# A written order of work up to head 16, weights decoded by half chunks, their remainders subtracted on GpSimd

## The chip, the cores and the metric

The kernel runs on one core of a Trainium2 chip. The metric is device time in microseconds (us). TensorE (PE) multiplies, VectorE (DVE), ScalarE (ACT) and GpSimd (POOL) do elementwise work, and the queue of SyncE (SP) issues most transfers. Each engine takes its instructions in the order in which they stand in its own queue; semaphores hold an instruction until what it needs is there.

## What is computed

A local window attention, followed by a feed-forward network over its output. There are 8 batches of 8 heads; the 512 queries of a head see 32 global keys and the keys at most 32 positions away, and the 32 global queries see all keys.

```python
s_l = np.concatenate([s_lg, np.where(mask, s_ll, -1e9)], axis=-1)
out_l = np.matmul(sm(s_l), np.concatenate([v_g, v_l], axis=2))
out_g = np.matmul(sm(s_g), v_all)
...
h = x @ w_in                      # x: 4608 x 512, w_in: 512 x 2048
r = np.maximum(h, 0.0)
g = s * (r * r) + b
return g @ w_out                  # w_out: 2048 x 512
```

The data are float32. The weights arrive as 64-bit floats; attention data as 32-bit ones.

## The kernel before

Most matmuls run on pairs: a float32 number is written as a rounded high part (`fp32r`) and the remainder, a low part, and three products are summed. So almost every operand is copied rounded on ACT and then subtracted from the original on DVE or POOL.

**Weights.** `w_in` and `w_out` come in 16 chunks each. A chunk k (`weight_load`) is two transfers of 512 KB into one staging tile `wst`: 1024 words of `w_in`, 1024 of `w_out`. `weight_words` turns half a chunk (128x512 numbers) from 64-bit words into pairs in five instructions: ACT rescales the high words (L157), DVE shifts them (L160) and joins the low words' bits to them (L161), ACT rounds the high part into `w_all` (L166), DVE subtracts it from the joined number (L167). These names below are *exponents*, *shift*, *join*, *round* and *subtract*. There are 32 halves.

**Steps.** The loop over j takes one half (256 queries) of one head at a time; "head j" is meant so. The first sixteen (NF = 16) use plain float32 matmuls on PE, the later ones use pairs. For a head: scores on PE into the one PSUM tile `ps_s`; mask and smallest value on DVE (L223, two instructions); exponentials on ACT (L229); a small addition and a reciprocal on DVE (L232, L233); division by the sum (L237 on ACT for one block and L239 on DVE for the other, as `NORM_ACT` says); four transpositions on PE into the one PSUM tile `turned` (L309, L311), a copy back on ACT (L326), and for each second head the product with the values (L339) and its copy to `x` (L347 on DVE, from head 8 on L345 on ACT). After eight heads `x_split` makes a pair of `x` and the feed-forward products can begin: in step j = m + 10 (LAG = 10) `ffn_in(m)` issues 24 matmuls (L515), relu on ACT, square on DVE (L522), a rounded copy on ACT (L529) and the remainder on DVE (L530), and `ffn_out` follows a step later with 12 matmuls (L547). There are 136 m.

**Who sets the order.** The loop is written in order of j, but a scheduler puts the instructions into the queues by its own estimates of time, with priorities: the float32 heads run under a priority 50 places ahead (`AHEAD`). One chunk is decoded at each j from 0 to 15 (`DECODED_AT`). In step j < 10 four matmuls on constants (`keep_busy`, L105) go ahead of the scores; 14 of them stand at the very start. The softmax tile `sm` has two buffers, staging tiles lie in the places of tiles that are used later (`SPOTS`: xs0, xs1 and two places of kq).

Of the kernel before, what the change touches and what calls it, by code (L numbers as in the profile page):

```python
# [48 lines left out]
WARM_UNTIL = 10  # L49
# [3 lines left out]
SPOTS = ["xs0", "xs1", "kq", "kq"] * 2 + ["xs1", "kq", "kq"] * 2 + ["xs1", "kq"]  # L53
DECODED_AT = list(range(16))
BY_HALVES = 16
NORM_ACT = lambda j, blk: j < NF and blk == 0
X_ACT = lambda j: j >= 8
# [4 lines left out]
GL_POOL = lambda m: False  # L62
# [8 lines left out]
def window_attention_then_ffn(ctx: ExitStack, tc: tile.TileContext, qd, qg, kw, vw, vg, qz, qgz, vz, w_in, w_out, sv, bv, out):  # L71
# [75 lines left out]
    def weight_chunk(k):  # L147
        st = staged.pop(k)
        n = 2 if k < BY_HALVES else 1
        for i in range(n):  # L150
            c = 1024 // n
            weight_words(k, st[:, 2 * c * i:2 * c * (i + 1)], slice(c * i, c * (i + 1)))

    def weight_words(k, st, at):
        words = st.rearrange("p (n w) -> p n w", w=2)
        low, high = words[:, :, 0], words[:, :, 1]
        nc.scalar.activation(  # L157
            out=high.bitcast(F32), in_=high.bitcast(F32), func=AF.Prelu, scale=2.0**-112, alpha=2.0**32,
        )
        nc.vector.tensor_scalar(out=high, in0=high, scalar1=3, scalar2=None, op0=ALU.logical_shift_left)  # L160
        nc.vector.scalar_tensor_tensor(  # L161
            out=low, in0=low, scalar=29, in1=high, op0=ALU.logical_shift_right, op1=ALU.bitwise_or,
        )
        m = low.bitcast(F32)
        hi, lo = (w_all[:, i, k].rearrange("p w c -> p (w c)")[:, at] for i in range(2))
# [25 lines left out]

    def split(j):
# [14 lines left out]
    def v_split(j):  # L207
# [3 lines left out]
        nc.scalar.copy(out=vs[:, :, 0, :], in_=rv4)  # L211
# [394 lines left out]
    for j in range(NM + LAG + 2):  # L606
# [12 lines left out]
        if j < NS:  # L619
# [106 lines left out]
```

## Time and profile before

| | |
|---|---|
| time, median of 3 runs | 1012.91 us (1012.5 to 1012.93) |
| the profiled execution: its time, its span | 1012.75 us, 1010.9 us |
| busy in the span: PE, weight loads of PE | 994.8 us (98%), 906.0 us |
| DVE, ACT, POOL | 804.0 us, 695.4 us, 288.5 us |
| granted clock of PE, mean | 0.998 of 2.4 GHz |
| transfers | 82.05 MB; 332, 342 and 278 GB/s in the first three of 40 equal slices, 36 to 106 in most later ones |

The span runs from the first to the last instruction; the time holds 1.85 us more. Engines overlap, so busy times are not to be added. An instruction's record lasts until its result is written; the next of its engine starts a little earlier.

### The profile page before, as it was taken

What the parts mean: (1) busy time and instruction counts of PE and PEld (TensorE: products, weight loads), DVE (VectorE), ACT (ScalarE), POOL (GpSimd) and SP (SyncE); (2) the same over time, 40 slices, a digit from 0 to 9 for tenths busy, and PEclk for the clock granted to TensorE, in tenths of its full rate; (3) what the DMA queues carried; (4) which work ended last, traced back from release to release, by engine and by line L of the source; (5) the groups of instructions that cost most, each with busy time, mean ns of one, the idle gap of its engine ahead of it and who ended that gap; (6) DMA issues with size and microseconds to landing.
All of it is one profiled execution on the core that took longest, in us unless ns stands there. A gap on an engine that the chain in (4) does not pass through costs nothing.

```text
span 1010.9 us, 20088 instructions
## 1 busy us (share of the span) xinstructions
PE 994.8 (98%) x6940; PEld 906.0 (90%) x6942; DVE 804.0 (80%) x2097; ACT 695.4 (69%) x1801; POOL 288.5 (29%) x366
## 2 busy tenths in 40 slices
PE   8699999999999999999999999999999999999998
PEld 5589999999999999999999999999999999999887
DVE  7998678888789778988789789988789788964322
ACT  7997667768677667868677667867678667743222
POOL 1002224424243224424244224424234223401000
PEclk9999999999999999999999999999999999999999
DMA  9982212313132212313132112312132112101000
GB/s 332 342 278 77 73 48 66 93 45 99 45 91 66 65 48 62 106 34 93 49 94 69 58 55 62 98 41 87 44 104 69 55 55 65 62 1 49 23 22 21
DMA packets 63845, 82.05 MB, mean 81 GB/s; under 512 B 7680, under 2 KB 51200, under 8 KB 63744
## 3 DMA queue, kind: packets, MB, share of 16 engines
q1 hardware_dynamic: 63168, 79.46, 25.8%
q8 instruction: 55, 0.90, 0.4%
q10 hardware_dynamic: 576, 1.31, 0.4%
q14 instruction: 46, 0.38, 0.1%
HBM read 71.30 MB, written 9.44 MB: 80 GB/s over the span
## 4 chain that ended last, share of the span: by engine, by line
PE 91%; DVE 4%; ACT 3%; issue 1%; DMA 1%; DVEq 0%; ACTq 0%
PE ps_h L515 36%; PE acc L547 35%; PE ps_s L373 5%; PE ps_o L401 4%; PE turned L311 3%; PE turned L309 3%; PE ps_og L467 2%; PE ps_g L380 1%; PE turned L445 1%; PE ps_s L284 1%; DVE wst L161 1%; PE ps_o L339 1%; DVE sm L223 1%; ACT sm L229 0%; DVE wst L160 0%
## 5 line engine op out<-in xcount | busy, mean ns | idle before, releaser
L515 PE MATMUL ps_h<-xst,w_all 128*128 128x256 f32 x3264 | 437.6, 281 | 1.0 <-ACT xst L500 0.7
L547 PE MATMUL acc<-w_all,g 128*128 128x512 f32 x1632 | 422.3, 396 | 0.0
L515 PEld LDWEIGHTS ps_h<-xst,w_all 128*128 128x128 f32 x3264 | 408.0, 189 | 8.9 <-ACT xst L500 0.9
L547 PEld LDWEIGHTS acc<-w_all,g 128*128 128x128 f32 x1632 | 289.9, 188 | 49.6
L212 POOL TENSOR_TENSOR vs<-rv,vs 128x192 fp32r<-128x192 f32 x112 | 70.8, 632 | 301.2 <-ACT vs L211 288.6
L229 ACT ACTIVATE sm<-sm,nm 128x224 f32<-128x224 f32 x256 | 121.5, 477 | 34.3 <-DVE nm L223 33.0
L522 DVE SCALAR_TENSOR_TENSOR r<-ps_h,s_t,r 128x512 f32<-128x512 f32 x136 | 101.5, 746 | 52.7 <-ACT r L521 50.9
L530 DVE SCALAR_TENSOR_TENSOR g<-r,b_t,g 128x512 fp32r<-128x512 f32 x136 | 111.1, 817 | 38.7 <-ACT g L529 34.6
L204 POOL TENSOR_TENSOR kq<-rq,kq 128x256 fp32r<-128x256 f32 x112 | 91.8, 820 | 161.4 <-ACT kq L203 151.3
L529 ACT ACTIVATE g<-r,b_t 128x512 fp32r<-128x512 f32 x136 | 98.5, 724 | 55.1 <-DVE r L522 54.9
L521 ACT ACTIVATE r<-ps_h 128x512 f32<-128x512 f32 x136 | 81.2, 597 | 67.6 <-PE ps_h L515 57.5
L459 POOL TENSOR_TENSOR vsg<-rvg,vsg 128x320 fp32r<-128x320 f32 x64 | 56.8, 908 | 125.5 <-ACT vsg L458 124.1
L239 DVE TENSOR_SCALAR sm<-sm,nm 128x224 f32<-128x224 f32 x240 | 87.8, 405 | 4.0
L373 PE MATMUL ps_s<-kq 128*128 128x224 f32 x448 | 73.7, 275 | 0.0
L373 PEld LDWEIGHTS ps_s<-kq 128*128 128x128 f32 x448 | 67.1, 190 | 6.1
L390 ACT CAST pt<-turned 128x416 fp32r<-128x416 f32 x112 | 57.4, 513 | 21.6 <-PE turned L311 21.0
L391 DVE TENSOR_TENSOR pt<-turned,pt 128x416 fp32r<-128x416 f32 x112 | 65.5, 585 | 7.0 <-ACT pt L390 6.3
L385 DVE TENSOR_TENSOR sg<-ps_g,tg 32x256 f32<-32x256 f32 (+1 forms) x112 | 48.2, 430 | 22.4 <-ACT tg L384 17.0
L309 PE MATMUL turned<-ident,sm 128*96 128x128 f32 (+1 forms) x256 | 63.7, 274 | 1.8 <-DVE sm L239 1.2
L384 ACT COPY tg<-ps_g 32x256 f32<-32x256 f32 (+1 forms) x112 | 42.1, 376 | 32.3 <-PE ps_g L380 29.6
L311 PE MATMUL turned<-ident,sm 128*128 128x128 f32 x256 | 63.1, 273 | 0.0
L401 PE MATMUL ps_o<-pt,vs 128*128 128x256 f32 x336 | 62.9, 295 | 0.0
(81 smaller groups left out, 1273.6 us busy)
## 6 DMA issues: line engine op xcount, KB each, us to landing
rq<-in_qd SPq DMA_DIRECT2D x112, 128.0 KB, 2.2
rk<-in_kw SPq DMA_DIRECT2D x64, 176.0 KB, 2.3
rv<-in_vw SPq DMA_DIRECT2D x112, 96.0 KB, 1.9
rvg<-in_vg SPq DMA_DIRECT2D x32, 320.0 KB, 3.0
out<-o SPq DMA_DIRECT2D x32, 256.0 KB, 2.2
wst<-in_w_in SPq DMA_DIRECT2D x15, 512.0 KB, 5.2
wst<-in_w_out SPq DMA_DIRECT2D x15, 512.0 KB, 6.0
rv<-in_vz SPq DMA_DIRECT2D x16, 192.0 KB, 4.5
```

Source lines behind the costliest of these rows:

```text
L204: nc.gpsimd.tensor_sub(out=qs[:, 1, :], in0=rq, in1=f32(qs[:, 0, :]))
L229: nc.scalar.activation(out=p, in_=p, func=AF.Exp, bias=nm[:, blk:blk + 1], scale=-1.0, accum_out=ss[:, blk:blk + 1],)
L239: nc.vector.tensor_scalar(out=p, in0=p, scalar1=ss[:, blk:blk + 1], scalar2=1.0, op0=ALU.mult, op1=ALU.mult,)
L309: nc.tensor.transpose(out=p_t[0:n, s0:s0 + P], in_=sm[:, c0:c0 + n], identity=ident)
L311: nc.tensor.transpose(out=p_t[:, o0:o0 + P], in_=sm[:, c0:c0 + P], identity=ident)
L373: nc.tensor.matmul(p_s[:, W * blk:W * blk + W], lhsT=qs[:, a, blk * P:(blk + 1) * P], rhs=ks[:, KEYS[blk]], start=(a == 0), stop=(a == 1),)
L401: nc.tensor.matmul(p_o[:, :, q], lhsT=vs[0:n, c], rhs=pt[0:n, :, o], start=(c == 0), stop=(c == 1))
L515: nc.tensor.matmul(p_h[:, k], lhsT=wi[:, a, f, c], rhs=xs[:, e, c, :], start=(n == 0), stop=(n == 11),)
L522: nc.vector.scalar_tensor_tensor(out=r, in0=p_h, scalar=s_t, in1=r, op0=ALU.mult, op1=ALU.mult)
L529: nc.scalar.activation(out=g[:, 0], in_=r, func=AF.Identity, bias=b_t)
L530: nc.vector.scalar_tensor_tensor(out=g[:, 1], in0=r, scalar=b_t, in1=f32(g[:, 0]), op0=ALU.add, op1=ALU.subtract,)
L547: nc.tensor.matmul(oacc[t][i], lhsT=g[:, a, k, i * P:(i + 1) * P], rhs=wo[:, e, f, :], start=(pr == 0 and n == 0), stop=(pr == 7 and n == 5),)
```

## The change

The first sixteen heads get a loop of their own, `first_steps(j)`, whose instructions stand in ACT's, DVE's, PE's and SP's queues as they are written (`tc.manual_schedule`); POOL's are scheduled as before. A step j now issues: exponentials of head j, mask and smallest of head j+1, first half of the feed-forward products of m = j-10, scores of head j+2, copy back and value product of head j-1, then the first half chunk of the step mixed with the sums and the division of head j, its transpositions, the second half of the products, the 12 output products of m-1, and then further half chunks. `HALVES_AT` says how many halves a step decodes: one in steps 3 to 7, two in 8 and 9, four in 10 to 14, three in 15. The subtraction of a half is issued on POOL (`half_low`), one half behind; when the second half of chunk k is done, chunk k+3 is loaded into its place (three places). Both divisions of a head and all copies of value products to `x` are on DVE. `sm` takes a third buffer in the place of `g` for three heads (2, 5, 8). Fillers ahead of the scores end with head 4, not 9. Instructions of ACT and of `x_split` up to head 18 keep the written order among themselves (`behind`); after head 15 the old loop goes on under the scheduler.

```diff
-WARM_UNTIL = 10
+WARM_UNTIL = 5
-SPOTS = ["xs0", "xs1", "kq", "kq"] * 2 + ["xs1", "kq", "kq"] * 2 + ["xs1", "kq"]
-DECODED_AT = list(range(16))
-NORM_ACT = lambda j, blk: j < NF and blk == 0
-X_ACT = lambda j: j >= 8
+SPOTS = ["xs0", "kq", "kq"] + ["xs1", "kq", "kq"] * 4 + ["xs1"]
+HALVES_AT = {3: 1, 4: 1, 5: 1, 6: 1, 7: 1, 8: 2, 9: 2, 10: 4, 11: 4, 12: 4, 13: 4, 14: 4, 15: 3}
+KEPT = 19
+X_ACT = lambda j: False
...
-        nc.vector.tensor_sub(out=lo, in0=m, in1=f32(hi))
+    def half_low(h):
+        if h >= 0:
+            low, high, hi, lo = half(h)
+            nc.gpsimd.tensor_sub(out=lo, in0=low.bitcast(F32), in1=f32(hi))
+            if h % 2:
+                staged.pop(h // 2)
+                if h // 2 + 3 < 16 and h // 2:
+                    weight_load(h // 2 + 3)
...
+    def first_steps(j, halves):
+        m = j - LAG if j >= LAG else None
+        pending = [halves.pop(0) for _ in range(HALVES_AT.get(j, 0))]
...
+        if f and m:
+            ffn_relu(m - 1)
+        exponentials(j)
...
+            least(j + 1, st_.pop(("ps", j + 1)))
+        if f:
+            ffn_products(m, 0)
+        if j + 2 < NF:
+            scores32(j + 2)
+        if j:
+            turned32(j - 1)
+            pv_products32(j - 1)
...
+        if f and m:
+            ffn_square(m - 1)
+            ffn_high(m - 1)
+        h = pending.pop(0) if pending else None
+        if h is not None:
+            half_exponents(h + 1)
+            half_shift(h)
+        if j > 1:
+            pv_copy32(j - 2)
+        sums(j)
+        if h is not None:
+            half_low(h - 1)
+        inverses(j)
+        if f and m:
+            ffn_low(m - 1)
+        if h is not None:
+            half_join_words(h)
+        divide(j)
+        p_transposes(j)
+        if h is not None:
+            half_high(h)
+        if f:
+            ffn_products(m, 1)
+            if m:
+                ffn_out(m - 1)
+        n = 0
+        while pending:
+            decode(*g_at.pop((j, n), ()))
+            n += 1
+        if j in SPLIT_AT:
+            x_split(SPLIT_AT[j])
...
+    with tc.manual_schedule(engines={mybir.EngineType.Activation, mybir.EngineType.DVE, mybir.EngineType.PE, mybir.EngineType.SP}):
```

`decode` issues, for each further half h of a step: exponents of h+1, shift of h, subtract of h-1, join of h, round of h.

On DVE, before, this is a stretch from the middle of the sixteen heads, in which two subtractions of one chunk stand between the shifts and joins of the next (L223 and L239 of heads around them are as above; `gm`, `sg` are the softmax of the global queries):

```order
L160 TENSOR_SCALAR wst_425<-wst_425 128x512
L167 TENSOR_TENSOR w_all<-wst_371,w_all 128x512
L233 RECIPROCAL nm_489<-nm_489 128x2
L160 TENSOR_SCALAR wst_425<-wst_425 128x512
L161 SCALAR_TENSOR_TENSOR wst_425<-wst_425 128x512
L232 TENSOR_SCALAR nm_541<-nm_541 128x2
L239 TENSOR_SCALAR sm_488<-sm_488,nm_489 128x224
L161 SCALAR_TENSOR_TENSOR wst_425<-wst_425 128x512
```

On DVE now, this is step 11 from the square of m = 0 (L623) on; L631 is the feed-forward remainder, L164 the join, L272 the two divisions of head 11:

```order
L623 SCALAR_TENSOR_TENSOR r_631<-ps_h_555,s_t,r_631 128x512
L160 TENSOR_SCALAR wst_534<-wst_534 128x512
L403 COPY x_516<-ps_o_572 128x256
L258 TENSOR_SCALAR nm_552<-nm_552 128x2
L262 RECIPROCAL nm_552<-nm_552 128x2
L631 SCALAR_TENSOR_TENSOR g_660<-r_631,b_t,g_660 128x512
L164 SCALAR_TENSOR_TENSOR wst_534<-wst_534 128x512
L272 TENSOR_SCALAR sm_551<-sm_551,nm_552 128x224 x2
L160 TENSOR_SCALAR wst_611<-wst_611 128x512
L164 SCALAR_TENSOR_TENSOR wst_611<-wst_611 128x512
L160 TENSOR_SCALAR wst_611<-wst_611 128x512
L164 SCALAR_TENSOR_TENSOR wst_611<-wst_611 128x512
```

No subtraction is left there, four shifts and four joins stand in a step, three pairs of them side by side at its end. On POOL, before, the first work after the masks at the start of the program is that of the global values (L459, L364) and of head 16 (L204, L202):

```order
L114 AFFINE_SELECT mask_high<-mask_high 128x192
L459 TENSOR_TENSOR vsg_0_1202<-rvg_0_1200,vsg_0_1202 128x5x64 x2
L364 TENSOR_TENSOR qgs_1064<-rqg_966,qgs_1064 128x8x32
L204 TENSOR_TENSOR kq_1031<-rq_954,kq_1031 128x256
L202 TENSOR_TENSOR kq_1031<-rk_952,kq_1031 64x352
```

On POOL now, at the same place (L179 is the subtraction of a half, two to a chunk; the first and the last of sixteen rows):

```order
L112 AFFINE_SELECT mask_high_63<-mask_high_63 128x192
L179 TENSOR_TENSOR w_all_60<-wst0_145,w_all_60 128x512 x2
...
L179 TENSOR_TENSOR w_all_60<-wst15_1003,w_all_60 128x512 x2
L223 TENSOR_TENSOR kq16_1108<-rq16_726,kq16_1108 128x256
```

So 32 instructions of 128x512 have come in ahead of head 16's. On PE, before, this is the place of head 14's transpositions (L309, L311 of `sm_971`); 159 matmuls of L515 and 60 of L547 stand ahead of it in the queue:

```order
L547 MATMUL acc_0_761<-w_all,g_1009 128x512 x4
L547 MATMUL acc_1_762<-w_all,g_1009 128x512 x4
L515 MATMUL ps_h_1164<-xst_609,w_all 128x256 x13
L309 MATMUL turned<-ident,sm_971 128x128
L311 MATMUL turned<-ident,sm_971 128x128
```

On PE now, this is the place of head 15's transpositions (L355, L357 of `sm_927`), the last of the sixteen; L603 is the first product, L647 the output product, and 156 and 48 of them stand ahead:

```order
L647 MATMUL acc_1_690<-w_all,g_957 128x512 x6
L603 MATMUL ps_h_1026<-xst_539,w_all 128x256 x12
L603 MATMUL ps_h_1155<-xst_539,w_all 128x256 x24
L355 MATMUL turned<-ident,sm_927 128x128
L357 MATMUL turned<-ident,sm_927 128x128
L355 MATMUL turned<-ident,sm_927 128x128
L357 MATMUL turned<-ident,sm_927 128x128
L603 MATMUL ps_h_1026<-xst_539,w_all 128x256 x12
L647 MATMUL acc_0_689<-w_all,g_1042 128x512 x6
L647 MATMUL acc_1_690<-w_all,g_1042 128x512 x6
L388 MATMUL ps_o_1100<-pt_1039,rv_952 128x128 x2
```

In the written order the second half of a step's products and its output products stand behind the transpositions of that step's head.

## Rows read from the trace of the kernel before

**Rows 1.** Busy time of each engine in two stretches, clock, share and rate of transfers.
```profile
20.00:53.00 33.00, 24.60 (x126) 16.82 (x125) 32.99 (x103) 32.08 (x81) 1.98 (x2) 0.95 1.00 346
53.00:88.00 35.00, 35.00 (x239) 32.09 (x237) 34.94 (x87) 32.03 (x76) 4.05 (x4) 1.00 0.62 204
```

**Rows 2.** Timeline of PE: start and length in us, engine, line, tiles, count.
```profile
6.08 0.92 PE L284 MATMUL ps_s<-rk,rq 128*128 128x224 f32 x4
6.83 1.03 PE L105 MATMUL warm<-warm 128*128 128x512 bf16 x4
...
53.14 0.56 PE L515 MATMUL ps_h<-xst,w_all 128*128 128x256 f32 x2
...
94.18 0.27 PE L309 MATMUL turned<-ident,sm 128*128 128x128 f32 x1
```

**Rows 3.** The chain that ended last, in order of time: start, length, what.
```profile
61.70 2.73 PE ps_h L515 x24
...
98.81 0.44 PE turned L445 x4
...
104.59 2.73 PE acc L547 x12
```

**Rows 4.** Timeline of DVE, a stretch without gaps.
```profile
68.60 0.68 DVE L167 TENSOR_TENSOR w_all<-wst,w_all 128x512 fp32r<-128x512 f32 x1
69.20 0.16 DVE L232 TENSOR_SCALAR nm<-nm 128x2 f32<-128x2 f32 x1
69.27 0.42 DVE L160 TENSOR_SCALAR wst<-wst 128x512 int32<-128x512 int32 x1
69.61 0.68 DVE L161 SCALAR_TENSOR_TENSOR wst<-wst 128x512 int32<-128x512 int32 x1
70.21 0.33 DVE L239 TENSOR_SCALAR sm<-sm,nm 128x224 f32<-128x224 f32 x1
70.46 0.74 DVE L522 SCALAR_TENSOR_TENSOR r<-ps_h,s_t,r 128x512 f32<-128x512 f32 x1
```

**Rows 5.** Groups of DVE by shape, 0 to 100 us: busy us, mean ns.
```profile
L223 DVE CUSTOM_DVE_ANT_0 sm<-ps_s,mask_mid 128x224 f32<-128x224 f32 x17 | 6.6, 385 | 0.0
L429 DVE TENSOR_REDUCE gm<-sg 128x1 f32<-128x544 f32 x2 | 1.4, 716 | 0.0
```

**Rows 6.** Timeline of POOL, three places.
```profile
26.15 1.98 POOL L459 TENSOR_TENSOR vsg<-rvg,vsg 128x320 fp32r<-128x320 f32 x2 [22.40 <-ACT vsg L458]
...
78.88 0.99 POOL L204 TENSOR_TENSOR kq<-rq,kq 128x256 fp32r<-128x256 f32 x1 [12.47 <-ACT kq L203]
79.95 1.01 POOL L202 TENSOR_TENSOR kq<-rk,kq 64x352 fp32r<-64x352 f32 x1
...
90.83 0.74 POOL L204 TENSOR_TENSOR kq<-rq,kq 128x256 fp32r<-128x256 f32 x1 [0.22 <-ACT kq L203]
```

**Rows 7.** Timeline of DVE at the same three places.
```profile
26.46 0.95 DVE L239 TENSOR_SCALAR sm<-sm,nm 128x224 f32<-128x224 f32 x1
27.33 1.35 DVE L161 SCALAR_TENSOR_TENSOR wst<-wst 128x512 int32<-128x512 int32 x1
...
78.85 1.31 DVE L160 TENSOR_SCALAR wst<-wst 128x512 int32<-128x512 int32 x2
80.07 1.43 DVE L167 TENSOR_TENSOR w_all<-wst,w_all 128x512 fp32r<-128x512 f32 x1
...
90.67 0.74 DVE L522 SCALAR_TENSOR_TENSOR r<-ps_h,s_t,r 128x512 f32<-128x512 f32 x1
```

**Rows 8.** The page's groups of POOL: busy us, mean ns, idle before.
```profile
L212 POOL TENSOR_TENSOR vs<-rv,vs 128x192 fp32r<-128x192 f32 x112 | 70.8, 632 | 301.2 <-ACT vs L211 288.6
L459 POOL TENSOR_TENSOR vsg<-rvg,vsg 128x320 fp32r<-128x320 f32 x64 | 56.8, 908 | 125.5 <-ACT vsg L458 124.1
```

**Rows 9.** Timeline of PE, scores of a head at 49 us.
```profile
48.83 1.65 PE L284 MATMUL ps_s<-rk,rq 128*128 128x224 f32 x4 [0.51 <-DVE nm L223]
```

**Rows 10.** The page's transfers: KB each, median us from issue to landing.
```profile
wst<-in_w_in SPq DMA_DIRECT2D x15, 512.0 KB, 5.2
```

More of the change, by code (lines that the diff above doesn't have):

```diff
@@ L145, in weight_load, with half, half_exponents, half_shift @@
             queue.dma_start(st[:, 1024 * i:1024 * (i + 1)], sources[i])
[L147 to L159, printed above, removed]
+    def half(h):
+        k, i = h // 2, h % 2
+        words = staged[k][:, 1024 * i:1024 * (i + 1)].rearrange("p (n w) -> p n w", w=2)
+        hi, lo = (w_all[:, a, k].rearrange("p w c -> p (w c)")[:, 512 * i:512 * (i + 1)] for a in range(2))
+        return words[:, :, 0], words[:, :, 1], hi, lo
+    def half_exponents(h):
+        if h < 32:
+            high = half(h)[1]
+            nc.scalar.activation(
+                out=high.bitcast(F32), in_=high.bitcast(F32), func=AF.Prelu, scale=2.0**-112, alpha=2.0**32,
+            )
+    def half_shift(h):
+        high = half(h)[1]
         nc.vector.tensor_scalar(out=high, in0=high, scalar1=3, scalar2=None, op0=ALU.logical_shift_left)
+    def half_join_words(h):
+        low, high, hi, lo = half(h)
         nc.vector.scalar_tensor_tensor(
@@ L190, in v_load, with behind @@
         st_["rv", j] = rv
+    def behind(j, done):
+        if j < KEPT:
+            tc.keep_in_program_order(done)
     def split(j):
@@ new lines, in ffn_products, with ffn_in @@
+        if k == 0:
+            st_["h", m] = ps.tile([P, 2, HALF], F32, tag="h", name=f"ps_h{m}", bufs=2)
+        p_h = st_["h", m]
+        f = 2 * pr + k
+        n = 0
+        for c in range(4):
+            for a, e in ((0, 0), (0, 1), (1, 0)):
+                nc.tensor.matmul(
+                    p_h[:, k], lhsT=wi[:, a, f, c], rhs=xs[:, e, c, :],
+                    start=(n == 0), stop=(n == 11),
+                )
+                n += 1
+    def ffn_in(m):
+        ffn_products(m, 0)
+        ffn_products(m, 1)
+        ffn_relu(m)
+        ffn_square(m)
+        ffn_high(m)
+        ffn_low(m)
@@ L535, in window_attention_then_ffn, with ffn_low @@
+    def ffn_low(m):
+        g = gs_[m]
+        nc.vector.scalar_tensor_tensor(
+            out=g[:, 1], in0=st_.pop(("r", m)), scalar=b_t, in1=f32(g[:, 0]), op0=ALU.add, op1=ALU.subtract,
+        )
     oacc = {}
@@ L583, in run, with pick @@
+    assert not halves and not staged and not g_at, (halves, g_at)
+    def pick(one):
         def run(j):
@@ L652, in window_attention_then_ffn @@
             late.pop(j)()
-    assert piece == 16 and not extra
+    assert not extra
 def kernel(**inputs):
```

269 lines of the change are left out of this document (168 added, 101 removed).

## The prediction

> **What bounds the kernel now.** Read the busy times by stretch first [rows 1]. From 53 us on PE is busy throughout, and it stays so to the end, at full clock: from there the time is PE's own work, and nothing on another engine counts. From 20 to 53 us PE is busy 24.6 of 33 us, a good part of it in gaps between small matmuls, while DVE is busy 32.99 and ACT 32.08: there the decoding of weights and the softmax set the pace. So the change can win only by bringing PE to its dense work earlier, and lose by starving it later. On PE's timeline [rows 2] the reader is to see two marks: at 53.14 the feed-forward products begin in earnest (12 of their matmuls ran before), and at 94.18 head 14 is transposed. Between them DVE was busy all but 0.06 of 35 us, yet PE never waited for it [rows 1].
>
> **A common mark.** I compare both programs at one amount of PE work: the place where the new order has head 15's transpositions. Ahead of it stand 156 first and 48 output products; before, at 94.18, 159 and 60 had been issued. Twelve output products take 2.73 us, 24 first ones 2.73 and four transpositions 0.44 [rows 3]. Before had done 12 output products (2.73) and 3 first products (0.34) more, and had still to do one head's transpositions (0.44) and half a value product (some 0.7, six matmuls of the first products' length). So its clock at this mark is 94.2 - 3.1 + 1.1 = 92.3 us. If the new program starts these transpositions at T and starves no more after it, its time is 1012.75 + T - 92.3, since all of PE's work behind the mark is the same.
>
> **DVE's lane up to the mark.** The transpositions wait for head 15's division on DVE. DVE's stretch without gaps [rows 4] gives the cost of an instruction as start to start of the next, about 0.08 us less than its record: subtract 0.60, sum 0.07, shift 0.34, join 0.60, division 0.25, square 0.66 (its record is 0.74). The smallest-value instruction is then 0.31 and the global maximum 0.63 [rows 5]. Up to the division of head 15 DVE has in the new order:
> - 16 heads, each two smallest (0.62), sum and reciprocal (0.14), two divisions (0.50): 1.26, together 20.2 us. One division per head has come over from ACT, 4 us of these.
> - 7 copies of value products, some 0.33 each by their 256 columns: 2.3.
> - 30 halves of shift and join, 0.94 each: 28.2. The 0.60 of each subtraction, 19 us over 32 halves, are gone.
> - the pair of `x`, two at 0.60: 1.2; five squares and five remainders at 0.66: 6.6; global softmax with two maxima: 1.9.
>
> That is 60.4 us. It begins with the first smallest value: scores stood at 6.08 and took 0.75 [rows 2]; four fillers now stand ahead of them (0.9 by the next start on PE), and the result has to land: 8.0 us. DVE then has idle time that the order makes. In steps 0 to 2 no weights are decoded, and each step waits for PE's fillers, scores and the single score tile, some 2.7 us a step: 8.0 us for 4.4 us of DVE work, so 3.6 idle (bounds 2 and 5). Steps 3 to 7, with one half each, take 2.4 us of DVE, and ACT has about as much (four of its instructions for the head, two for the half); for ACT setting the pace I allow 1.5 (bounds 0 and 3), and for the feed-forward chain through ACT 1.0 (0 to 2). I chose these, no row gives them. Without the subtractions the mark comes at 8.0 + 60.4 + 6.1 = 74.5 us by DVE.
>
> **The subtractions on POOL.** No row shows one of 512 columns. By the groups of 192 and 320 columns [rows 8] a column costs (908 - 632) / 128 = 2.16 ns, so one takes 908 + 192 x 2.16 = 1320 ns, and 29 of them 38 us, which POOL has. But they are not free for DVE. At three places DVE runs beside POOL [rows 6, 7]. At 26 us two subtractions of POOL follow each other for 1.98 us: DVE's division takes 0.95 and not 0.33, its join 1.35 and not 0.68 [rows 4], 1.29 us lost. At 78.9 us two more: two shifts take 1.22 from start to next start and not 0.68, the subtraction 1.43 and not 0.68, again 1.29 lost. At 90.8 us the square, which reads PSUM and one tile of SBUF, takes its 0.74 beside POOL and loses nothing. So DVE's instructions with two SBUF inputs, and those like shift and division, wait until POOL's is done, and lose 0.64 of a record of 0.99. A queued instruction of POOL gets in after just one of DVE's. For 512 columns I take 1.0 us (1.32 less 0.35; in proportion to columns 1.03; bounds 0, wholly hidden, and 1.3).
>
> The Trainium skill, page "SBUF — State Buffer", section "SBUF: two separate sides", states that DVE's second port pair is an exclusive lock with GpSimd, held for the whole instruction, by whichever starts first. The trace agrees that one waits for the other, at 0.64 of 0.99 us; by the page's whole instruction an exposed subtraction would cost 1.32, and the time would come out at 1023 (a rival below).
>
> How many are exposed? In steps 10 to 14 a step's last join is followed by the next step's two smallest values and (from 11 on) the square, 1.28 us of instructions that do not wait: one subtraction hides there, with 0.2 to 0.4 left over. The other three of a step fall between shift, join and division. That is 15 in steps 10 to 14, 1 between the divisions of step 15, and 3 in steps 8 and 9 with the pair of `x` behind them. Nineteen at 1.0 and 2.3 left over: 21.3 us, where the subtractions on DVE itself had cost 19. T = 74.5 + 21.3 = 95.8 us.
>
> **What is late next.** PE reaches the feed-forward products at about 41 us (8.0 + 24 of the 60.4 + 5 idle + 4 for POOL), 12 us earlier than before. But steps 11 to 14 then last 6.5 us of DVE's work (1.4 for the head, 1.3 for the feed-forward network, four times 0.94) plus 3.3 lost, 9.8, where PE has 2.73 + 2.73 of products and 1.9 of attention (scores 0.75, transpositions 0.44, half a value product 0.7): it waits 2.4 us a step. Behind the mark PE has 0.44 + 1.4 + 2.73 us; then the value product of head 15 waits for its copy on ACT, which stands behind the rounded copy of m = 5, and that behind two halves and the square on DVE, some 5.5 us: 1 us more. Other edits: the third score buffer only lets three early heads run ahead, in steps that PE or ACT sets; three staging places are enough at 9.8 us a step: between the subtraction that frees a place and the exponents that need its next content lie three of a step's four halves and the step's other work, some 0.8 of it or 8 us, and a subtraction of 1.3 and a landing of 5.2 [rows 10] fit. Both at nothing; if steps were short, the second would count (below).
>
> Sum: 1012.75 + 95.8 + 1.0 - 92.3 = **1017.2 us**, against 1012.75 for the profiled execution and 1012.91 for the median; I say 1017.
>
> **Rivals.**
> - *The subtractions hide.* If POOL's work falls into DVE's waits, or costs it little, DVE's 74.5 is not the bound; PE is: from 39 us on it has 156 x 0.114 + 48 x 0.2275 + some 11 us of attention = 39.7, and 2 of small waits, so T = 81 and the time 1002. For it: POOL was idle in this stretch but for 2 us. Against it: [rows 7]. The point that decides is the average cost of a subtraction to DVE: 74.5 + 29 c + 1 = 92.3 at c = 0.58 us, against 0.73 in my sum. At c = 0.4 it is 1007.
> - *Loads set the pace.* A place is free only when POOL has subtracted. With steps of 7.5 us, those 0.8 are 6 us, and subtraction and landing take 1.3 + 5.2: 0.5 to 0.8 a step lost, some 4 us. This needs the first rival and makes it 1006.
> - *PE's clock falls earlier.* Before, with no fillers among them, scores took 1.65 us at 48.83 and not 0.92 [rows 2, 9]; the clock was at half, and over 20 to 53 us its mean was 0.95 of full [rows 1]. The fillers now end with head 4, at about 15 us; if the clock falls in step 6 or 7 and holds until the products, each step's 1.9 us of PE work takes 3.8, up to 1 us above ACT's pace: 2 to 3 us, 1020.
> - *A blocked instruction loses the whole of POOL's.* If each exposed subtraction costs its 1.32 us, the 19 cost 6 more: 1023. Its 0.64 of 0.99 in [rows 7] speaks against it. The Trainium skill's page named above would have it so.
> - *Written order with more stalls.* A step's waits across engines are exposed one by one; at 0.7 us in each of steps 8 to 15, 1022.
>
> **Chances.** My sum, T between 92 and 98 (1014 to 1020): 0.46. Subtractions partly hidden, 1007 to 1014: 0.20. Wholly hidden, with or without late loads, below 1007: 0.17. Clock, stalls or whole instructions on top, above 1020: 0.17 (0.06, 0.05, 0.06). The range that leaves out 0.2 is 1004 to 1022; the likeliest case alone spans 1014 to 1020. A measurement of this kernel tells about 0.2% from no change, here 2 us. Faster by more than that (below 1010.9): 0.17 and most of 0.20, 0.31. Within it: 0.16. Slower: 0.53.
>
> **What the profile after would show.** Right: first dense products near 41 us; shift, join or division near 1.3 to 1.6 us beside a POOL record of 1.3; DVE full from 16 to 98 us; PE idle some 2.5 us ahead of each of the transpositions of heads 11 to 15, waiting for the division; those of head 15 at about 96 us; from 105 us on the same chain of products as before. Wrong: joins at 0.68 throughout, or PE without idle time after 45 us, then the first rival; waits of ACT's exponents for `wst`, then the loads; scores of heads 8 to 11 at 1.6 us per four, then the clock.

## The result, and the profile after

The changed kernel takes **1027.12 us** (median of 4 runs, 1026.79 to 1027.66) against 1012.79 for the kernel before on the same chip: a ratio of 1.0142, 95% interval 1.0125 to 1.016. It is slower by 14.3 us, where 4 were forecast. In its profiled execution (1027.29 us, span 1025.4) head 15's transpositions, the mark of the prediction, stand at 105.17 us and not at 95.8, and the first dense products at 47.2 and not at 41:

Timeline of PE of the changed kernel (start, length, line, tiles):
```profile
47.21 0.58 PE L603 MATMUL ps_h<-xst,w_all 128*128 128x256 f32 x1 [0.41 <-ACT xst L574]
...
105.17 0.30 PE L355 MATMUL turned<-ident,sm 128*128 128x128 f32 x1 [0.93 <-DVE sm L272]
```
Behind the mark lie 920.2 us (1025.4 - 105.2), before 918.6 (1010.9 - 92.3): 1.6 us lost there, 12.9 ahead of it. Three stretches of the changed kernel, to be read against [rows 1] (engines PE, PE's loads, DVE, ACT, POOL, then granted clock, DMA share, GB/s):
```profile
42.00:54.00 12.00, 8.44 (x33) 6.84 (x33) 11.31 (x24) 8.58 (x19) 4.59 (x5) 0.57 0.60 209
54.00:64.00 10.00, 6.52 (x49) 5.57 (x48) 9.86 (x20) 7.18 (x16) 5.18 (x4) 1.00 0.81 262
64.00:74.00 10.00, 9.89 (x57) 8.95 (x57) 9.80 (x19) 7.49 (x17) 5.35 (x4) 0.83 0.74 252
```
From 53 us on, where PE was busy throughout before, it now has holes, and DVE is still full. The granted clock means 0.57 from 42 to 54 us: half its level, 1.2 GHz, for most of it, in a stretch that begins with small scores and long holes. One step of the dense part shows the cause of the holes. DVE's timeline:
```profile
74.11 0.42 DVE L160 TENSOR_SCALAR wst<-wst 128x512 int32<-128x512 int32 x1
74.57 1.70 DVE L164 SCALAR_TENSOR_TENSOR wst<-wst 128x512 int32<-128x512 int32 x1
76.19 0.42 DVE L160 TENSOR_SCALAR wst<-wst 128x512 int32<-128x512 int32 x1
76.64 1.70 DVE L164 SCALAR_TENSOR_TENSOR wst<-wst 128x512 int32<-128x512 int32 x1
...
78.57 0.38 DVE L242 CUSTOM_DVE_ANT_0 sm<-ps_s,mask_high 128x224 f32<-128x224 f32 x1
...
78.88 0.74 DVE L623 SCALAR_TENSOR_TENSOR r<-ps_h,s_t,r 128x512 f32<-128x512 f32 x1
79.55 0.52 DVE L160 TENSOR_SCALAR wst<-wst 128x512 int32<-128x512 int32 x1
...
81.84 1.64 DVE L272 TENSOR_SCALAR sm<-sm,nm 128x224 f32<-128x224 f32 x2
```
and POOL's, with the page's group of its subtractions (busy, mean ns):
```profile
74.33 1.39 POOL L179 TENSOR_TENSOR w_all<-wst,w_all 128x512 fp32r<-128x512 f32 x1 [1.33 <-DVE wst L164]
76.41 1.39 POOL L179 TENSOR_TENSOR w_all<-wst,w_all 128x512 fp32r<-128x512 f32 x1 [0.69 <-ACT wst L154]
78.47 1.31 POOL L179 TENSOR_TENSOR w_all<-wst,w_all 128x512 fp32r<-128x512 f32 x1 [0.68 <-DVE wst L164]
82.06 1.29 POOL L179 TENSOR_TENSOR w_all<-wst,w_all 128x512 fp32r<-128x512 f32 x1 [2.28 <-DVE wst L164]
...
L179 POOL TENSOR_TENSOR w_all<-wst,w_all 128x512 fp32r<-128x512 f32 x32 | 42.7, 1333 | 63.3 <-DVE wst L164 28.6
```
Two joins take 1.70 and not 0.68 [rows 4], the two divisions 1.64 and not 0.58; the third subtraction lies beside a smallest value and the square, which keep their 0.38 and 0.74, and leaves 0.1 over for the shift (0.52 for 0.42). Three of four exposed, one hidden, 1.01 to 1.06 us each: as forecast. PE waits for the division, as the waits of PE from 47 to 106 us show (us in all, times, longest):
```profile
PE turned L355 <- DVE sm L272: 7.6, 4, 3.0
```

### The profile page after: what moved, and what is told of

It reads as the page before. It is cut to its first block, busy times and chain, and to the rows that moved or that the text cites. A ratio compares the mean times of both kernels' runs of the same rounds, so it can differ in the third digit from the quotient of the medians.

```text
span 1025.4 us, 20027 instructions
## 1 busy us (share of the span) xinstructions
PE 999.6 (97%) x6921; PEld 910.2 (89%) x6922; DVE 814.1 (79%) x2085; ACT 689.9 (67%) x1781; POOL 331.5 (32%) x398
## 4 chain that ended last, share of the span: by engine, by line
PE 87%; DVE 8%; issue 2%; ACT 2%; DMA 1%; SPq 0%; POOL 0%; DVEq 0%; POOLq 0%; ACTq 0%
PE ps_h L603 34%; PE acc L647 34%; PE ps_s L429 4%; PE ps_o L457 4%; PE turned L355 2%; PE turned L357 2%; PE ps_og L554 2%; DVE sm L272 1%; PE ps_g L436 1%; DVE wst L160 1%; DVE wst L164 1%; PE warm L103 1%; PE turned L530 1%; DMA rq<-in_qz 1%; DVE r L623 1%
## 5 line engine op out<-in xcount | busy, mean ns | idle before, releaser
L603 PE MATMUL ps_h<-xst,w_all 128*128 128x256 f32 x3264 | 438.7, 282 | 3.8 <-DVE r L623 1.3
L647 PE MATMUL acc<-w_all,g 128*128 128x512 f32 x1632 | 422.4, 397 | 0.0
L603 PEld LDWEIGHTS ps_h<-xst,w_all 128*128 128x128 f32 x3264 | 409.7, 190 | 11.8 <-DVE xst L575 1.7
L647 PEld LDWEIGHTS acc<-w_all,g 128*128 128x128 f32 x1632 | 291.0, 189 | 50.4
L623 DVE SCALAR_TENSOR_TENSOR r<-ps_h,s_t,r 128x512 f32<-128x512 f32 x136 | 101.4, 746 | 58.1 <-ACT r L619 56.9
L631 DVE SCALAR_TENSOR_TENSOR g<-r,b_t,g 128x512 fp32r<-128x512 f32 x136 | 111.4, 819 | 37.7 <-ACT g L627 33.3
L223 POOL TENSOR_TENSOR kq<-rq,kq 128x256 fp32r<-128x256 f32 x112 | 92.7, 828 | 142.1 <-ACT kq L222 128.1
L272 DVE TENSOR_SCALAR sm<-sm,nm 128x224 f32<-128x224 f32 x256 | 99.0, 429 | 3.9
L546 POOL TENSOR_TENSOR vsg<-rvg,vsg 128x320 fp32r<-128x320 f32 x64 | 56.7, 907 | 105.3 <-ACT vsg L543 105.2
L355 PE MATMUL turned<-ident,sm 128*96 128x128 f32 (+1 forms) x256 | 64.0, 275 | 12.2 <-DVE sm L272 11.9
L179 POOL TENSOR_TENSOR w_all<-wst,w_all 128x512 fp32r<-128x512 f32 x32 | 42.7, 1333 | 63.3 <-DVE wst L164 28.6
L357 PE MATMUL turned<-ident,sm 128*128 128x128 f32 x256 | 63.1, 273 | 0.0
```

The source lines that it names most:

```text
L223: nc.gpsimd.tensor_sub(out=qs[:, 1, :], in0=rq, in1=f32(qs[:, 0, :]))
L272: nc.vector.tensor_scalar(out=p, in0=p, scalar1=ss[:, blk:blk + 1], scalar2=1.0, op0=ALU.mult, op1=ALU.mult,)
L355: nc.tensor.transpose(out=p_t[0:n, s0:s0 + P], in_=sm[:, c0:c0 + n], identity=ident)
L357: nc.tensor.transpose(out=p_t[:, o0:o0 + P], in_=sm[:, c0:c0 + P], identity=ident)
L603: nc.tensor.matmul(p_h[:, k], lhsT=wi[:, a, f, c], rhs=xs[:, e, c, :], start=(n == 0), stop=(n == 11),)
L623: nc.vector.scalar_tensor_tensor(out=r, in0=p_h, scalar=s_t, in1=r, op0=ALU.mult, op1=ALU.mult)
```

## The experiments

The times are medians; "mark" is head 15's transpositions in the profiled execution, one of those behind the median. Kernel before: 1012.8 to 1013.5 beside these, mark 92.3 (reckoned in the prediction, its order having no such place). Behind the mark lie 919.9 to 921.4 us in most versions; where it is more, the text says so.

| kernel | us | ratio to before, 95% | first dense, mark |
|---|---|---|---|
| changed | 1027.1 | 1.0142 (1.0125 to 1.016) | 47.2, 105.2 |
| sub_dve | 1020.5 | 1.007 (1.005 to 1.009) | 42.7, 93.5 |
| sub_none | 1013.3 | 1.0005 (0.9995 to 1.0014) | 44.4, 90.5 |
| pool_copy | 1015.7 | 1.0024 (1.0008 to 1.0041) | 45.3, 93.4 |
| before_pool | 1025.0 | 1.0118 (1.0103 to 1.0133) | |
| mix | 1017.8 | 1.0048 (1.0033 to 1.0063) | 45.5, 95.2 |
| sp_free | 1033.5 | 1.0203 (1.0188 to 1.0218) | 53.2, 111.2 |
| fill10 | 1025.3 | 1.0122 (1.0107 to 1.0137) | 45.1, 103.1 |
| early | 1030.4 | 1.0173 (1.0158 to 1.0188) | 56.4, 108.0 |
| mix_early | 1022.3 | 1.01 (1.0082 to 1.0118) | 52.8, 100.0 |
| none_act | 1013.3 | 0.9996 (0.9986 to 1.0006) | 43.6, 90.6 |
| none_halves | 1012.9 | 0.9989 (0.998 to 0.9999) | 41.7, 87.5 |
| none_short | 1011.4 | 0.9977 (0.9967 to 0.9987) | 44.5, 88.5 |
| short_act | 1009.7 | 0.996 (0.9945 to 0.9974) | 41.9, 86.5 |
| mix_halves | 1016.2 | 1.0026 (1.0017 to 1.0036) | 43.9, 93.7 |
| spill2 | 1026.9 | 1.0138 (1.012 to 1.0156) | 41.9, 97.8 |
| spill4 | 1026.0 | 1.0125 (1.0108 to 1.0142) | 41.8, 98.6 |
| spill_halves | 1021.1 | 1.0072 (1.0057 to 1.0087) | 41.6, 90.5 |
| best | 1019.4 | 1.0057 (1.0044 to 1.007) | 43.5, 93.2 |

### What the subtractions cost, and by what

**sub_dve**, subtractions on DVE:
```diff
-            nc.gpsimd.tensor_sub(out=lo, in0=low.bitcast(F32), in1=f32(hi))
+            nc.vector.tensor_sub(out=lo, in0=low.bitcast(F32), in1=f32(hi))
```


> The changed kernel with each subtraction on DVE and not on POOL, at the same place of the order. Port theory (a subtraction on POOL holds DVE up, and nearly all of them do, not 19): a subtraction costs DVE 0.60 us here instead of 1.0 to 1.07, some 26 exposed ones: 26 x 1.05 = 27 go, 29 x 0.60 = 17.4 come, about 10 us faster than the changed kernel, 1017, and no join at 1.69 is left. Rival (the price was 21.3 as forecast, the miss comes from late loads and the half clock ahead of the first dense products): 21.3 - 17.4 = 4 us faster, 1023. Second rival (what POOL takes from DVE is nothing, the waits come from the written order alone): DVE gets 17.4 us more work, slower, 1035 to 1044.

It came between the first two, 6.6 us faster than the changed kernel: DVE with 17 us more work is better off than with POOL beside it. By the medians the written order with DVE's own subtractions costs 7.1 us against before, POOL as much again (ratios 1.007 and 1.0142). Its executions spread from 1018.0 to 1022.5; the one with a trace is the fastest, and its mark, 93.5, is 11.7 us earlier, near what the first line has.

**sub_none**, no subtractions:
```diff
-            nc.gpsimd.tensor_sub(out=lo, in0=low.bitcast(F32), in1=f32(hi))
...
-                    lhsT=wi[:, a, f, c], rhs=xs[:, e, c, :],
+                    lhsT=wi[:, 0, f, c], rhs=xs[:, e, c, :],
...
-                        oacc[t][i], lhsT=g[:, a, k, i * P:(i + 1) * P], rhs=wo[:, e, f, :],
+                        oacc[t][i], lhsT=g[:, a, k, i * P:(i + 1) * P], rhs=wo[:, 0, f, :],
```


> The changed kernel without its 32 subtractions; the products take the rounded high part of the weights where they took the low part, so that PE's work is the same in number and shape. It measures what the subtractions cost in all. Port theory with some 26 exposed at 1.05: 27 us of the 105.2 at head 15's transpositions go, so that PE, not DVE, sets most of the stretch: those transpositions at 79 to 82 us, time 1001 to 1004. Rival (21.3 as forecast, the rest of the miss is loads and clock, which stay): transpositions at 84 to 88, time 1006 to 1010. Second rival (the written order alone): transpositions later than 98, 1020 or more.

All three missed. The groups of DVE up to the mark of the changed kernel (busy us, mean ns) say what POOL does to DVE,
```profile
L164 DVE SCALAR_TENSOR_TENSOR wst<-wst 128x512 int32<-128x512 int32 x30 | 29.6, 986 | 0.5
L272 DVE TENSOR_SCALAR sm<-sm,nm 128x224 f32<-128x224 f32 x32 | 17.8, 599 | 0.1
L160 DVE TENSOR_SCALAR wst<-wst 128x512 int32<-128x512 int32 x31 | 17.2, 556 | 0.0
```
beside those without subtractions (lines below L179 are one lower there):
```profile
L164 DVE SCALAR_TENSOR_TENSOR wst<-wst 128x512 int32<-128x512 int32 x30 | 20.6, 687 | 0.5
L160 DVE TENSOR_SCALAR wst<-wst 128x512 int32<-128x512 int32 x31 | 13.2, 425 | 0.2
L271 DVE TENSOR_SCALAR sm<-sm,nm 128x224 f32<-128x224 f32 x32 | 9.3, 332 | 0.1
```
30 x 0.299, 8.5 and 4.0 make 21.5 us, and the pair of `x` and the global division lose another 1.4: 23 us, against 21.3 forecast. But the mark moves by 14.7 only, from 105.2 to 90.5, and the time ends where it was before the change: **with subtractions at no price at all, the written order gains nothing.**

**pool_copy**, POOL copies (one input) instead of subtracting; products as in sub_none:
```diff
-            nc.gpsimd.tensor_sub(out=lo, in0=low.bitcast(F32), in1=f32(hi))
+            nc.gpsimd.tensor_copy(out=lo, in_=low.bitcast(F32))
```


> The changed kernel with POOL copying the joined words into the low part instead of subtracting (one SBUF input in place of two; the products take the high part twice, PE's work is the same). If any instruction of POOL on SBUF holds DVE's shift, join and division up, these are stretched by about the copy's own length and the time is 1019 to 1027 according to that length. If only two-input instructions do, nothing is stretched and it is 1013 to 1015, as without subtractions.

By the time alone it looks nearly like the second; its trace says the first, with a short instruction. DVE's and POOL's timelines:
```profile
76.20 1.03 DVE L164 SCALAR_TENSOR_TENSOR wst<-wst 128x512 int32<-128x512 int32 x1
...
77.61 1.03 DVE L164 SCALAR_TENSOR_TENSOR wst<-wst 128x512 int32<-128x512 int32 x1
...
75.78 0.91 POOL L179 CAST w_all<-wst 128x512 fp32r<-128x512 f32 x1 [1.26 <-DVE wst L164]
77.30 0.79 POOL L179 CAST w_all<-wst 128x512 fp32r<-128x512 f32 x1 [0.61 <-DVE wst L164]
```
A join beside a copy of 0.79 loses 0.34; beside a subtraction of 1.39 it lost 1.01. Both joins end 0.55 us after POOL's record, 0.14 less than the 0.69 that they take alone: DVE's instruction is held until shortly before the end of POOL's, and what it loses depends on how long POOL's had been running when it started (0.31 us here, 0.24 there).

**before_pool**, this part of the change alone, in the kernel before:
```diff
-        nc.vector.tensor_sub(out=lo, in0=m, in1=f32(hi))
+        nc.gpsimd.tensor_sub(out=lo, in0=m, in1=f32(hi))
```


> The kernel before with one part of the change alone: its 32 subtractions on POOL, everything else in the scheduler's hands. The written order with subtractions on DVE cost 7.3 us (1020.5 against 1013.2), the whole change 14.3. If the two parts add up, this costs 7: 1018 to 1022, with shifts, joins and divisions of 1.3 to 1.7 us. If a scheduler that sees DVE's other work hides them (first rival of the forecast), DVE loses 19 us of work for less than that: 1005 to 1012.

12.0 us slower, with no written order at all, and above both lines. DVE's and POOL's timelines:
```profile
45.10 1.26 DVE L232 TENSOR_SCALAR nm<-nm 128x2 f32<-128x2 f32 x1
46.40 0.17 DVE L233 RECIPROCAL nm<-nm 128x2 f32<-128x2 f32 x1
46.48 1.40 DVE L160 TENSOR_SCALAR wst<-wst 128x512 int32<-128x512 int32 x1
...
44.60 2.99 POOL L167 TENSOR_TENSOR w_all<-wst,w_all 128x512 fp32r<-128x512 f32 x2 [1.50 <-ACT w_all L166]
```
Even the sum over 128x2 numbers, 0.16 us otherwise, waits for POOL; the reciprocal behind it does not.

**mix**, only the subtractions that start beside the smallest values stay on POOL:
```diff
-            half_low(h - 1)
+            half_low(h - 1, nc.gpsimd if j >= 11 else nc.vector)
```
(all others take `nc.vector`, the last of all POOL.)

> The changed kernel with only six subtractions left on POOL, the first of each of the steps 11 to 15 and the last of all, which start beside the smallest values and the square; the other 26 are on DVE in their place. Port theory: against all of them on DVE (1020.5; transpositions of head 15 at 93.5) five times 0.60 less, and 1 us back for what is left over of the hidden ones: 91.5, time 1012 to 1016. Rival (ACT, with some 8 us of work a step, sets steps 11 to 14 once DVE is lighter, as with no subtractions at all: transpositions at 90.5 there): the same number but no further gain from any lightening of DVE. Rival (a subtraction on POOL costs DVE 1.0 wherever it stands): 1021 or more.

2.7 us faster than sub_dve by the medians, but the intervals of the two ratios overlap: the direction of the first line is not shown, and the time is 1.8 us above its range. The third line's 1021 is refuted. Its mark, 95.2, is later than sub_dve's in an execution whose first smallest value came at 9.4 us and not at 8.0 (in sub_none at 9.4, in the changed kernel at 8.9): marks carry such scatter, 7.9 to 9.6 over all versions.

### The steps ahead of the first dense products

**sp_free**: `mybir.EngineType.SP` taken out of the engines with a written order.

> The changed kernel with SP's queue, which issues the loads, put back into the scheduler's hands; the queues of PE, DVE and ACT stay as written. If late loads from the written order of SP are a good part of the miss (the load of head 8's queries came 7.1 us after its issue, scores waited), the first dense products come 3 to 5 us before 47.2 and the time is 1022 to 1024. If DVE under the port is all of it, the time stays at 1026 to 1028.

Neither: 6.4 us slower. DVE waits 18.8 us for scores instead of 11.2; the written order of the loads is better than the scheduler's.

**fill10**: `WARM_UNTIL = 10`.

> The changed kernel with the fillers ahead of the scores up to head 9, as before the change. If the half clock at 29.9 to 33.3 and 43.5 to 53.8 us costs time, both go and it is 2 to 4 us faster, 1023 to 1025. If DVE sets the pace there anyway, the fillers' 0.9 us a step in five steps change nothing or cost up to 2: 1027 to 1029.

1.8 us faster by the medians, at the edge of the first line; the intervals overlap, and of the mark's 2.1 us 0.6 are an earlier first smallest value (8.2). The fall of the clock at 30 us went, that from 42 to 54 us stayed (0.57 there too).

**early** (and `weight_load(j + 1)` in steps 0 to 2):
```diff
-HALVES_AT = {3: 1, 4: 1, 5: 1, 6: 1, 7: 1, 8: 2, 9: 2, 10: 4, 11: 4, 12: 4, 13: 4, 14: 4, 15: 3}
+HALVES_AT = {1: 1, 2: 1, 3: 2, 4: 2, 5: 2, 6: 2, 7: 2, 8: 2, 9: 2, 10: 3, 11: 3, 12: 3, 13: 2, 14: 4, 15: 1}
```


> The changed kernel with its half chunks spread over the steps from 1 on (one in steps 1 and 2, two in 3 to 9, three in 10 to 12, two in 13, four in 14, one in 15) and the loads of chunks 1 to 3 issued in steps 0 to 2; subtractions stay on POOL. If the miss is idle time of DVE ahead of the first dense products (11.9 us idle up to head 15's transpositions, forecast 6.1), 6 to 8 halves that now fill it are 5 to 8 us less at the end: 1019 to 1022. If loads or ACT set steps 3 to 9, those steps grow by what the later ones lose: 1025 to 1029.

Worse by 3.3 us: the first dense products come at 56.4, and the later steps win back 6.4 of those 9.2 us. An early half is not absorbed: in its trace shifts take 1.17 and pairs of divisions 1.64 us in these steps too, where its subtraction stands ahead of the division that the step waits for, and ACT waits 4.2 us for chunks.

**mix_early**, both and `WARM_UNTIL = 10`.

> Both of the former and fillers up to head 9: halves from step 1 on, 26 subtractions on DVE, six on POOL. If idle time of DVE, the port and the half clock are the whole of the loss, the gains add up: 1014 for the mix, less 4 to 7 for the earlier halves, 1 to 2 for the fillers: 1005 to 1010, faster than both kernels. If ACT's work (about 8 us a step in 11 to 14) or the loads are the next limit, 1011 to 1016.

4.4 us slower than the mix, first dense products at 52.8: the same with subtractions on DVE.

### What sets the written order's pace without subtractions

**none_act**, sub_none without the rounded copies of odd chunks:
```diff
-        nc.scalar.copy(out=hi, in_=high.bitcast(F32))
+        if h // 2 % 2 == 0:
+            nc.scalar.copy(out=hi, in_=high.bitcast(F32))
```
(products take chunk `f - f % 2`.)

> The kernel without subtractions, with ACT lighter by half of the rounded copies of the weights (those of odd chunks are left out; the products take the neighbouring even chunk, the same number and shape). Without subtractions the time was 1013.3 and not the 1002 of the first rival. If ACT is what set steps 11 to 14 there (8.5 us each; DVE has 6.5 us of work, PE 7.4), two rounds less a step are 1.1 us: those steps 7.4 to 7.6 us, head 15's transpositions at 83 to 86, time 1004 to 1008. If it is loads or the waits of the written order as such, 1011 to 1014.

No change: ACT alone it is not. sub_none's chain that ended last has weight transfers in it (start, length):
```profile
51.80 6.12 DMA wst<-in_w_in
...
65.85 7.24 DMA wst<-in_w_out
```
**none_halves**, sub_none, with the load of half h+6 issued when half h is done:
```diff
-                if h // 2 + 3 < 16 and h // 2:
-                    weight_load(h // 2 + 3)
+            if h // 2 and h + 6 < 32:
+                half_load(h + 6)
```


> Without subtractions (as before, products take the high part twice), and each staging place freed by halves: the load of half h+6 is issued as soon as half h is done, where both transfers of a chunk waited for its second half. Loads theory: a place's cycle is landing (5 to 6 us) plus the decoding of what lies in it; freeing by halves takes a quarter to half of a step of it, so steps 11 to 14 go from 8.5 to about 7.5 us, head 15's transpositions from 90.5 to 85 or 86: 1007 to 1010. If the waits of the written order as such set the pace: 1012 to 1014.

**none_short**, the same with 128 of 1024 columns loaded from chunk 4 on.

> The former with the loads of chunks 4 to 15 cut to an eighth of their bytes (what else lies in the places is decoded again, so that all engines have the same instructions). Loads theory: the chain without loads is PE's and ACT's, head 15's transpositions at 81 to 84, time 1002 to 1006, where the first rival of the forecast stood. If the written order's own waits set the pace: 1011 to 1014, as with whole loads.

Marks at 87.5 and 88.5, times 1012.9 and 1011.4: by their times both fall on the second lines. Loads are worth 2 us, not 10.

**short_act**, none_short and none_act together, and queries and keys loaded ahead of chunks 1 to 3.

> No subtractions, loads of chunks 4 to 15 cut to an eighth, the rounded copies of odd chunks left out (products take the neighbouring even chunk), and the loads of chunks 1 to 3 issued behind the queries and keys of their step. If ACT and the loads stand one behind the other, both gone leave PE: first dense products at 40 to 42, head 15's transpositions 41 us later at 81 to 84 (88.5 with loads alone gone), time 1002 to 1005. If the waits of the written order are the limit, 86 to 88 and 1008 to 1011.

By the time the second line, but the chain from 55 us on is PE's own work, as in the first:
```profile
44.95 1.49 PE ps_s L331 x4
...
55.02 1.38 PE ps_h L610 x12
56.39 2.73 PE acc L654 x12
59.13 1.42 PE ps_h L610 x12
60.54 0.76 PE ps_s L331 x4
```
The mark stands at 86.5, 44.6 us behind the first dense products at 41.9. PE is busy 42.4 of these 44.6 us, the first 8.1 of them at a lower mean clock (columns as above):
```profile
41.90:86.50 44.60, 42.42 (x281) 38.45 (x282) 40.23 (x109) 36.34 (x81) 0.00 (x0) 0.96 0.28 78
41.90:50.00 8.10, 7.76 (x48) 7.40 (x49) 7.27 (x22) 6.02 (x14) 0.00 (x0) 0.79 0.25 75
```
This is the lowest time measured with this order: 3.5 us below the kernel before, with 32 subtractions, half of ACT's rounding and most of the loads left out. Against none_short it gains 1.7 us, and that ahead of the first dense products (41.9 for 44.5; from there to the mark 44.6 and 44.0), where the order of the loads and the start (first smallest value at 8.6 for 9.2) differ as well: what ACT's lighter work has in it is not shown.

### Attempts at a faster kernel

**mix_halves**: mix, fill10 and places freed by halves.

> The mix (26 subtractions on DVE, six on POOL; 1017.8) with fillers up to head 9 and places freed by halves. DVE has some 8.3 us of work a step there, as long as the loads take; if both share the limit, 2 to 4 us: 1013 to 1016. If DVE alone is the limit, 1 us: 1016 to 1018.

1.6 us faster than the mix by the medians, at the edge between the two lines; the fastest version with all its work, and still 2.7 us slower than before.

**spill2** and **spill4**: two halves ahead of the first scores, then
```diff
+HALVES_AT = {5: 1, 7: 1, 8: 1, 9: 1, 10: 4, 11: 4, 12: 4, 13: 4, 14: 4, 15: 4}
...
+HALVES_AT = {8: 1, 9: 1, 10: 4, 11: 4, 12: 4, 13: 4, 14: 4, 15: 4}
```
and the rest with head 16.

> The kernel with 26 subtractions on DVE (mix), fillers up to head 9, and halves elsewhere: two decoded ahead of the first scores, where DVE was idle until 8.9 us; one in steps 5, 7, 8, 9; four in 10 to 15; the last two with head 16 under the scheduler. DVE's lane theory: 3 us of work fall into the idle start and 3 us go behind head 15's transpositions, where DVE is not the bound: these at 89 to 90 instead of 95.2, time 1009 to 1012. If the work behind them is not hidden, 3 us come back: 1012 to 1015. If the lane is not the bound of steps 0 to 10, no gain: 1016 to 1018.

> As the former with only one half in each of steps 8 and 9 ahead of the four a step, and four halves with head 16. The first dense products come about 7 us earlier than in the mix (45.5), near 38 to 40. DVE's lane theory: 1006 to 1010, faster than both kernels. If the four halves behind head 15 delay the products of steps 16 and 17, or ACT sets the steps, 1011 to 1016.

Both missed every line, by 9 and 10 us. Dense products come at 41.8, but then the weights are not there. Waits of ACT in spill4:
```profile
ACT wst L154 <- DMA wst<-in_w_in: 10.6, 4, 5.1
```
**spill_halves**, spill4 with places freed by halves:

> The kernel with two halves ahead of the first scores and the last four with head 16 (spill4, 1026.0; a third of its chain from 40 to 100 us were transfers of weights) and places freed by halves. Loads theory: the 5 us that ACT waited at once for a chunk, and most of the other waits for transfers (12.5 us in all) go, and head 15's transpositions come at 88 to 91 instead of 98.6; the rest is 4.7 us later than otherwise for the four halves behind: 1013 to 1018. If the waits of the order itself replace them: 1022 to 1026.

Between the two lines: the mark moves from 98.6 to 90.5 as the first had it, but 927.6 us lie behind it and not 920. In spill2 and spill4, which also leave halves to head 16, it is 927.2 and 925.1; that these halves cost the 5 to 7 us is likely, but was not tried apart.

**best**: mix_halves with the loads of short_act's order, `X_ACT = lambda j: j >= 10`, and no fillers ahead of the first scores.

> mix_halves (1016.2) with the loads of chunks 1 to 3 behind the queries and keys of their step, the copies to x on ACT from step 10 on (three of 0.33 us less on DVE), and no fillers ahead of the first scores (0.9 us earlier start). If the terms add up: 2 for the late queries of head 8, 1 for the copies, 0.9 for the start: 1012 to 1013, the time before. If DVE is the only limit from 44 us on and the early steps absorb the rest: 1014 to 1016.

In the profiled executions the mark is 0.5 us earlier than in mix_halves, the end 4.5 later (3.2 by the medians): the terms did not add up. Behind the mark PE starves and its clock falls (ten microseconds of it, columns as above):
```profile
115.00:125.00 10.00, 8.29 (x52) 7.82 (x53) 8.94 (x24) 7.12 (x22) 6.66 (x7) 0.66 0.23 68
```
Why it does so there and not in mix_halves, these runs don't show.

## Why the prediction was wrong

**The direction was right, the size was not:** +4 was forecast and +14.3 measured, outside the range. Of this 10 us, the mark accounts for 9.4 (105.2 for 95.8).

**Right: the subtractions.** Forecast 1320 ns on POOL, measured 1333. Forecast 1.0 us for an exposed one, three of four in a dense step; measured 1.01 to 1.06, three of four. In sum 23 for 21.3, but with luck in the count: instruction by instruction beside sub_none, 23 were exposed and not 19 (two more in steps 4 and 5, two in 8 and 9), at 0.95 on average, and the hidden ones left 0.8 over and not 2.3. The smallest value and the square did not wait, as said.

**Right: DVE's work.** 60.4 forecast; sub_none's timeline, added up start to start in the same way, has 61.3.

**Wrong: "DVE's lane up to the mark", the 6.1 us of idle time** ("I chose these, no row gives them"), and with it the 74.5 us without subtractions, which sub_none puts at 90.5. In the changed kernel the first smallest value comes at 8.9 (forecast 8.0); DVE is idle 3.6 us in steps 0 to 2, as forecast, but 3.4 in steps 3 to 9 (forecast 1.5) and 0.9 after; and in 50 places an instruction of DVE starts only after its forerunner's record has ended, where the lane had counted every start 0.08 us before that end: 4.0 us (in sub_dve, where a subtraction stands between most shifts and joins, only in 25: now a join often follows at once the shift whose result it needs). So 8.9 + 61.3 + 23.0 + 7.9 + 4.0 = 105.1. Of the 9.4 us, 5.8 are idle time and these hand-overs, 1.7 the subtractions, 0.9 each the start and the work.

In sub_none the same sum is 9.4 + 61.3 + 14.4 + 5.0 = 90.1: 23 us of waiting for POOL are gone, but idle time has grown by 6.5 and the hand-overs by 1.0. The 1.0 us allowed "for the feed-forward chain through ACT" (0 to 2) is 4.3 there, as the groups of the square and the remainder show behind the second bar, and next to nothing in the changed kernel, where DVE is late itself:
```profile
L622 DVE SCALAR_TENSOR_TENSOR r<-ps_h,s_t,r 128x512 f32<-128x512 f32 x5 | 3.7, 749 | 1.8 <-ACT r L618 1.8
L630 DVE SCALAR_TENSOR_TENSOR g<-r,b_t,g 128x512 fp32r<-128x512 f32 x5 | 3.7, 748 | 2.5 <-ACT g L626 2.5
```
Where DVE is the bound, the lane comes nearer: with 29 subtractions of 0.60 it gives 91.9, and sub_dve measured 93.5. A sum of gapless starts is a bound for a written order, not its time: heads hang together by smallest value, exponential, sum, reciprocal, division and transposition, each on another engine or on the result just written.

**Wrong: the first rival and its point of decision.** It gave 1002 if the subtractions were hidden and a break-even at 0.58 us apiece. sub_none measures a price of zero: 1013.3, no gain; the lowest time, short_act's, is 1009.7. The forecast had PE's part end at 81: products from 39 on, 39.7 us of work, 2 of waits. In sub_none they begin at 44.4, PE works 42.4 and waits 3.6 us (90.5); in short_act it is 41.9, 42.4 and 2.2 (86.5). So the waits were sized about right, and what was missing is the later beginning and 2.7 us of PE's own work, part of it the clock: 0.79 of 2.4 GHz in the first 8.1 us of short_act's stretch, where the scores of a head ran 1.49 us and not 0.76. That a chunk's place is free too late (second rival) was a right mechanism, worth some 2 us alone (none_short). Of the others, *the written order with more stalls*, at 0.05, is nearest to what happened; *PE's clock falls earlier* was right in kind, and its 2 to 3 us are 1.8 by fill10, with overlapping intervals, though a part of the fall stayed; *the whole of POOL's instruction* is refuted as a price, 1.01 us of 1.39. The Trainium skill, page "SBUF — State Buffer", section "Who interferes with whom", states that a DVE instruction with two SBUF inputs contends with one of GpSimd that reads SBUF, and that the loser blocks fully. The traces agree up to the last 0.11 to 0.20 us of POOL's record. The joins lose 0.34 us of a copy's 0.79 and 1.01 of a subtraction's 1.39, in both about 0.4 less than the record: they start 0.31 and 0.24 us after it begins and are let go 0.14 before it ends.

**Behind the mark** 1.0 was forecast, 1.6 measured.

**The two parts.** The written order with DVE's own subtractions costs 7.1 us by the medians; before_pool, POOL's part alone, 12.0; both 14.3. Why they don't add up was not tried apart. By the forecast's own terms the order with DVE's subtractions comes out at 1013.4 (91.9 at the mark), about even. In sub_dve's one execution with a trace (1018.0) the mark is indeed only 1.2 us behind the kernel before; 4.1 of its 5.3 us lie behind the mark (922.7 for 918.6), where PE, busy throughout before, has holes:
```profile
110.00:120.00 10.00, 7.81 (x57) 6.45 (x56) 8.21 (x30) 8.74 (x28) 4.52 (x6) 1.00 0.31 89
```
So by these two executions nearly all of the changed kernel's loss up to the mark came with POOL (93.5 for 105.2). What sub_dve's slower executions lose, no trace shows.

Open: what holds the first dense products back to 41.7 to 44.5 us in the versions without subtractions; what happens behind the mark in sub_dve and in best; and what the second division of a head on DVE costs, 4 us of the forecast's lane, which no version put back on ACT.

## What to carry to other kernels

Before moving elementwise work from DVE to POOL, look for one place in the trace where both run at once and read off what DVE's two-input, shift and division instructions lose there: here it was 1.0 us, POOL's record less some 0.3 to 0.4, and more than the 0.60 that DVE needs to do the work itself. When an order is to be written by hand, price its base by running it with the disputed work left out: a lane summed start to start, with 6 us allowed for idle time, was 16 us short here, and the whole gain had been in that. Allowances that no row gives belong in the range with their full width.

## What was not expected of the hardware

Not only instructions with two inputs on POOL hold DVE up: a copy on POOL with one input (0.79 us) lengthened a join from 0.69 to 1.03. In the changed kernel, pool_copy and before_pool alike, the held instruction's own time began 0.11 to 0.20 us before the end of POOL's record, whichever of the two operations POOL did. And an addition of DVE over 128x2 numbers took 1.26 us beside two subtractions of POOL in a row (2.99 us), where it takes 0.16: the size of DVE's instruction does not protect it, though the reciprocal of the same size beside the second subtraction kept its 0.17.
